# A warm-up buffer 64 bytes longer: moving two groups of tiles to another address modulo 256

## The chip, the cores and the metric

The kernel runs on one core of a Trainium2 chip. The metric is the device time of one execution in microseconds (us), lower is better. A change of less than 0.2% (1.3 us here) can hardly be told from no change.

## What is computed

A recurrent retention block feeds a SwiGLU feed-forward block. The shapes are B, H, S, D = 4, 8, 768, 64 and 3072 tokens, 512 model columns, 1536 hidden columns, all float32.

```python
for t in range(S):                      # retention, gamma by head
    state = gamma * state + k[:, :, t] (outer) v[:, :, t]
    y[:, :, t] = scale * q[:, :, t] @ state
x = y.transpose(0, 2, 1, 3).reshape(B * S, H * D)
g, val = x @ w_gate, x @ w_val
out = (g * sigmoid(g) * val) @ w_out
```

## The kernel before

**Stages.** The tokens are worked on in four segments of 768 (two halves of 384). Each segment has an attention part, an "up" part (the products with `w_gate` and `w_val`) and a "down" part (the products with `w_out`). The loops over the hidden dimension have 12 blocks `f` of 128. The first segment's up part is plain (`plain_part` L914 and `plain` L896); the three others use seven products of 128x384 for each `f` (`product`, L1062). Down is `down` (L1125): for each `f` six products, one for each token block, of 128 hidden columns by 512 output columns. While segment s is in its down stage, the attention of segment s+1 is mixed into it in twelve short blocks (`scores_of`, `mix_a`, `mix_b`, `mix_c`, all through `mm` at L766).

**Three passes to a product.** To get float32 accuracy from TensorE's float32r type, which takes one pass, operands are split by ScalarE, VectorE and GpSimd into three parts of float32r (`near_a` L967, `near_b` L970, `near_c` L973, and `far_a` to `far_c`), and each product is summed over the three parts. Those passes are the "single-pass products" of the change's title: L914, L896, L1062 and L1125. The small attention products are in float32.

**Operands and their tiles.** A pass has a stationary operand (loaded into the array, 128x128) and a moving operand (streamed past it).

| line | columns of the moving operand | moving tile | stationary tile | passes |
|---|---|---|---|---|
| L914 (`plain_part`) | 256 | `x0` | `oitem` | 144 |
| L896 (`plain`) | 384 | `x0` | `oitem` | 480 |
| L1062 (`product`) | 384 | `xa` or `xb` | `gitem`, and `oitem` for one product in seven | 1512 |
| L1125 (`down`) | 512 | `oitem` (from `w_out`) | `gitem` (the split `hT`) | 864 |

`gitem` and `oitem` come from two rings: `item` hands out the four slots g0 to g3 and the three slots o0 to o2 in turn (a `gitem` with number k lies in slot k mod 4). So in each down stage the blocks f = 2, 6 and 10 have their stationary tile in g2, and in the up stages one `gitem` in four lies there.

**Where the tiles lie.** The tiles are laid out in SBUF one after another in the order in which the program first names them, each rounded up to 32 bytes. `hT`, `x0` (its space is that of `xa`), `first` (that of `xb`), g0, g1 and g3 come first, then `loads`, `tmp`, `chunk_x`, `tab`, `local`, `last`, `states`, `warm`; o0, o1, o2 and g2 are first named later and come behind `warm`:

```python
states = consts.tile([P, 2, 2, NP, D], F32, name="states")
warm = place("warm", P + 16)
...
t = place(f"{kind}item{k}", {"g": 3 * 2 * TH, "o": 3 * DM}[kind], R12,
          tag=f"{kind}{k % slots}")
```

`warm` has 144 words (576 bytes) in each partition. It is used by the sixteen small products ahead of the work (`warm_up`, L1214). With the program's first tile at byte 16,512, the addresses modulo 256 are: `hT`, `x0`/`xa`, `first`/`xb`, g0, g1, g3: 128. o0, o1, o2 and g2 (201,536 and on): 64. All slices that the passes take start at a multiple of 512 bytes from a tile's start, so the tile's value is also the operand's.

**Order.** The order of all steps is written out by hand in `PLAN` (a list of some 2,370 names such as `3/D6.2`: segment 3, down, f = 6, token block 2); each engine works its part of that list in order. No name, wait or instruction depends on an address.

Of the kernel before, what the change touches and what calls it, by code (L numbers as in the profile page):

```python
# [17 lines left out]
P = 128  # L18
# [358 lines left out]
def tile_retnet_swiglu(  # L377
# [31 lines left out]
    def place(name, n, dtype=F32, **kw):  # L409
        return consts.tile([P, n], dtype, name=name, **kw)  # L410
# [15 lines left out]
    local = place("local", 2 * NP * HC + H + NP)  # L426
    last = place("last", 512)
    states = consts.tile([P, 2, 2, NP, D], F32, name="states")
    warm = place("warm", P + 16)

    def lay(sizes):
        at, out = 0, []
# [868 lines left out]
```

## Time and profile before

| | |
|---|---|
| time, median of 3 runs | 655.86 us (655.47 to 656.15) |
| the profiled execution | 656.0 us, of which the span from first to last instruction is 654.2 us |
| TensorE busy | 640.8 us, 98% of the span |
| granted TensorE clock, mean | 0.994 |
| VectorE, ScalarE, GpSimd busy | 490.0, 389.8, 271.4 us |

Stages on the span's clock: attention and plain up 0 to 134 us, down of segment 0 to 201, up to 291, down to 358, up to 443, down to 512, up to 599, down to the end.

In the rows below, a row of the timeline gives the start (us), the time from the first start to the last end (us), engine, line, operation, tiles, shape and count. Matmuls overlap: each record lasts from the pass's start until its results are written, so a row of n passes spans n - 1 distances between starts and one record's length.

### The profile page before, as it was taken

How to read it: one execution, taken by the hardware profiler on the slowest of the kernel's cores; microseconds unless marked ns; L12 is line 12 of the kernel's file. 1: busy time of each engine (PE TensorE's matmuls, PEld its weight loads, DVE VectorE, ACT ScalarE, POOL GpSimd, SP SyncE). 2: the span in 40 equal slices, each digit the busy share in tenths (PEclk: the TensorE clock that was granted, in tenths of full speed). 3: DMA queues.
4: the chain of work that ended last, by engine and by line, in shares of the span. 5: the costliest groups of instructions: out<-in, count | busy, mean ns of one | idle time of the engine just before them, and what ended most of it. 6: DMA issues, size and time to landing. Idle time of an engine off the chain costs nothing.

```text
span 654.2 us, 14042 instructions
## 1 busy us (share of the span) xinstructions
PE 640.8 (98%) x5576; PEld 580.7 (89%) x5576; DVE 490.0 (75%) x712; ACT 389.8 (60%) x860; POOL 271.4 (41%) x174
## 2 busy tenths in 40 slices
PE   6999999999999999999999999999999999999997
PEld 6999999977778999997778999998777999999885
DVE  4898688798898887675787868767498776778361
ACT  3688788576855555665766555555676554654211
POOL 0544356534445685730103765650103766562000
PEclk8999999999999999999999999999999999999999
DMA  9999897498867444178765640449677434304554
GB/s 325 362 350 345 320 348 275 169 370 277 272 227 277 168 145 170 33 216 258 241 232 209 205 150 15 172 151 304 189 260 251 164 142 168 115 0 162 185 201 146
DMA packets 50050, 140.13 MB, mean 214 GB/s; under 512 B 4928, under 2 KB 17472, under 8 KB 49984
## 3 DMA queue, kind: packets, MB, share of 16 engines
q1 hardware_dynamic: 49552, 138.57, 61.4%
q8 instruction: 44, 0.72, 0.4%
q10 hardware_dynamic: 432, 0.66, 0.3%
q14 instruction: 22, 0.18, 0.1%
HBM read 109.32 MB, written 29.88 MB: 213 GB/s over the span
## 4 chain that ended last, share of the span: by engine, by line
PE 87%; DVE 6%; ACT 2%; DMA 2%; issue 1%; POOL 1%; SPq 0%; ACTq 0%; DVEq 0%; POOLq 0%
PE bank L1062 40%; PE bank L1125 25%; PE bank L896 12%; PE bank L766 5%; PE bank L914 3%; ACT chunk_x L996 1%; DMA rawp<-in_w_gate_dram 1%; DVE gitem L970 1%; PE bank L721 1%; PE bank L636 1%; PE bank L692 1%; DVE oitem L983 1%; PE bank L707 1%; DVE gitem L407 1%; DVE xa L983 1%
## 5 line engine op out<-in xcount | busy, mean ns | idle before, releaser
L1125 PE MATMUL bank<-oitem,gitem 128*128 128x512 f32 x864 | 212.6, 399 | 2.8 <-DVE oitem L983 1.9
L1125 PEld LDWEIGHTS bank<-oitem,gitem 128*128 128x128 f32 x864 | 159.3, 188 | 41.8 <-DVE oitem L983 3.8
L973 POOL TENSOR_TENSOR gitem<-gitem 128x768 fp32r<-128x768 f32 x72 | 143.6, 2003 | 105.7 <-DVE gitem L970 102.9
L1062 PE MATMUL bank<-xa,gitem 128*128 128x384 f32 x864 | 162.5, 337 | 0.6 <-ACT tmp L1078 0.3
L1062 PEld LDWEIGHTS bank<-xa,gitem 128*128 128x128 f32 x864 | 150.9, 188 | 2.9 <-ACT tmp L1077 2.1
L973 POOL TENSOR_TENSOR oitem<-oitem 128x256 fp32r<-128x256 f32 (+1 forms) x60 | 66.6, 1114 | 72.8 <-DVE oitem L970 70.9
L970 DVE SCALAR_TENSOR_TENSOR gitem<-gitem,loads 128x768 fp32r<-128x768 f32 x72 | 80.8, 1139 | 14.1 <-ACT gitem L967 11.7
L967 ACT ACTIVATE gitem<-loads 128x768 fp32r<-128x768 f32 x72 | 59.3, 842 | 51.1 <-PE bank L1062 39.4
L1062 PE MATMUL bank<-xb,gitem 128*128 128x384 f32 x432 | 85.9, 336 | 0.2 <-POOL gitem L973 0.2
L896 PE MATMUL bank<-x,oitem 128*128 128x384 f32 x480 | 84.6, 337 | 0.8 <-POOL oitem L973 0.8
L896 PEld LDWEIGHTS bank<-x,oitem 128*128 128x128 f32 x480 | 82.9, 188 | 1.5 <-POOL oitem L973 1.1
L1062 PEld LDWEIGHTS bank<-xb,gitem 128*128 128x128 f32 x432 | 76.5, 188 | 1.1 <-POOL gitem L973 0.6
L970 DVE SCALAR_TENSOR_TENSOR gitem<-gitem,hT 128x768 fp32r<-128x768 f32 x48 | 49.1, 1027 | 28.1 <-ACT gitem L967 28.0
L967 ACT ACTIVATE gitem<-hT 128x768 fp32r<-128x768 f32 x48 | 39.9, 840 | 43.7 <-PE bank L1125 36.2
L996 ACT COPY chunk_x<-bank 64x128 f32<-64x128 f32 x144 | 35.4, 260 | 29.6 <-PE bank L766 20.6
L793 POOL TENSOR_TENSOR loads<-loads,tab 128x512 f32<-128x512 f32 x9 | 13.6, 1508 | 92.7 <-PE bank L766 78.5
L407 DVE SCALAR_TENSOR_TENSOR gitem<-gitem 128x768 fp32r<-128x768 f32 x48 | 46.8, 982 | 0.6
L1062 PE MATMUL bank<-xb,oitem 128*128 128x384 f32 x216 | 43.7, 338 | 0.0
L1062 PEld LDWEIGHTS bank<-xb,oitem 128*128 128x128 f32 x216 | 37.8, 188 | 0.4 <-POOL oitem L973 0.2
L970 DVE SCALAR_TENSOR_TENSOR oitem<-oitem,loads 128x256 fp32r<-128x256 f32 (+1 forms) x42 | 32.7, 783 | 3.4 <-ACT oitem L967 3.3
L979 POOL TENSOR_TENSOR oitem<-oitem 128x512 fp32r<-128x512 f32 x12 | 20.6, 1715 | 28.2 <-ACT oitem L976 20.6
L1079 DVE TENSOR_TENSOR hT<-bank,tmp 128x384 f32<-128x384 f32 x36 | 19.9, 553 | 14.7 <-PE bank L1062 14.4
(112 smaller groups left out, 787.1 us busy)
## 6 DMA issues: line engine op xcount, KB each, us to landing
loads<-wup SPq DMA_DIRECT2D x36, 896.0 KB, 4.7
oitem<-wdnt SPq DMA_DIRECT2D x36, 768.0 KB, 4.5
wdnt<-oitem SPq DMA_DIRECT2D x12, 768.0 KB, 4.6
wup<-first SPq DMA_DIRECT2D x9, 896.0 KB, 5.6
rawp<-in_w_gate_dram SPq DMA_DIRECT2D x12, 512.0 KB, 6.4
rawp<-in_w_val_dram SPq DMA_DIRECT2D x12, 512.0 KB, 5.8
rawp<-in_w_out_dram SPq DMA_DIRECT2D x12, 512.0 KB, 6.2
out_dram<-chunk_x SPq DMA_DIRECT2D x22, 256.0 KB, 2.2
```

The source lines that it names most:

```text
L407: stt(o, x, 1.0, y, op0=mul, op1=op)
L766: nc.tensor.matmul(o, a, b, start=start, stop=True, skip_group_check=True)
L896: nc.tensor.matmul(o, w[:, a, ts(b, P)], X0[:, a, i, NC - 1 - b], start=a == b == 0, stop=a == 2 and b == NC - 1, skip_group_check=True)
L914: nc.tensor.matmul(o, w[:, a, ts(b, P)], X0[:, a, :, NC - 1 - b, ts(j, P)], start=a == b == 0, stop=a == 2 and b == NC - 1, skip_group_che ...
L967: act(o[0], x, AF.Copy, scale=CUT / FAR)
L970: stt(o[1], f32(o[0]), -FAR, x, op0=mul, op1=add)
L973: op(o[2], f32(o[0]), f32(o[1]), op=add)
L979: op(o[1], f32(o[0]), x, op=sub)
L996: copy(cx[half[i], ds(2 * h, 2), c, half[z]], y.rearrange("p (b t) -> p b t", b=2))
L1062: nc.tensor.matmul(o, w[:, a, k], x[:, a, KH - 1 - k], start=start and a == k == 0, stop=a == 2 and k == KH - 1, skip_group_check=True)
L1079: lambda: copy(p5, wb), lambda: tt(h1, x, p5, op=add),
L1125: nc.tensor.matmul(banks[tok], hs[f][:, a, ds(i * TH + u * P, P)], wo[f][:, a], start=f == a == 0, stop=f == NF - 1 and a == 2, skip_group ...
```

## The change

`warm` gets 16 more words, 64 bytes, in each partition. The sixteen warm-up products and the memset that fills the buffer keep their code; the memset covers 160 words instead of 144. Everything that is laid out behind `warm` moves by 64 bytes: o0, o1, o2 and g2 go from 64 to 128 modulo 256. Nothing else changes, neither an instruction nor its order.

```diff
     states = consts.tile([P, 2, 2, NP, D], F32, name="states")
-    warm = place("warm", P + 16)
+    warm = place("warm", P + 32)
```

## The prediction, as put on record

> **What bounds the kernel now.** I read the page first, for the shares of the engines and the chain that ended last:
>
> ```profile
> span 654.2 us, 14042 instructions
> PE 640.8 (98%) x5576; PEld 580.7 (89%) x5576; DVE 490.0 (75%) x712; ACT 389.8 (60%) x860; POOL 271.4 (41%) x174
> PE 87%; DVE 6%; ACT 2%; DMA 2%; issue 1%; POOL 1%; SPq 0%; ACTq 0%; DVEq 0%; POOLq 0%
> ```
>
> TensorE (PE) is busy for 98% of the span and carries 87% of the chain. Next come the waits of PE (engine, line, what it waited for: us in total, times, longest):
>
> ```profile
> PE bank L1125 <- DVE oitem L983: 1.9, 2, 1.5
> PE bank L896 <- POOL oitem L973: 0.8, 1, 0.8
> PE bank L1062 <- ACT tmp L1078: 0.3, 1, 0.3
> ```
>
> They are small, so the time is PE's own pace: passes times the distance between the starts of two passes. The chain in order of time shows that pace over long stretches (start, us, what):
>
> ```profile
> 33.25 13.80 PE bank L914 x120
> 47.05 60.32 PE bank L896 x348
> 600.96 49.49 PE bank L1125 x213
> ```
>
> The last stage is a single run of 213 passes, 49.49 / 213 = 0.232 us each. Is that one pace, or a mixture? By the kernel's order of slots, the passes of f = 2, 6 and 10 have a moving tile (o) and a stationary tile (g2) that both lie at 64 modulo 256; in the nine other blocks the stationary tile lies at 128. In the last stage's order the 18 passes from about 625.0 us on are f = 6, and the 54 before them are other blocks. So I asked for the timeline of PE inside each:
>
> ```profile
> 612.62 12.06 PE L1125 MATMUL bank<-oitem,gitem 128*128 128x512 f32 x51
> 626.83 2.43 PE L1125 MATMUL bank<-oitem,gitem 128*128 128x512 f32 x10
> ```
>
> and for the records' lengths (minimum/median/maximum ns):
>
> ```profile
> L1125 PE MATMUL bank<-oitem,gitem x51: 393/398/398, 612.6 to 624.3; 128*128 128x512 f32 x51
> L1125 PE MATMUL bank<-oitem,gitem x10: 389/389/390, 626.8 to 628.9; 128*128 128x512 f32 x10
> ```
>
> A row of n passes spans n - 1 distances and one record. Unequal addresses: (12.06 - 0.398) / 50 = 0.2332 us. Equal addresses: (2.43 - 0.389) / 9 = 0.2268 us. Same shape, same line, same clock, nothing waiting in either: there are two paces, 6.4 ns apart, and today three quarters of the down passes (648 of 864) have the longer one. This is the observation on which the forecast rests.
>
> **The up passes (384 columns).** Here the moving tile lies at 128, g0, g1 and g3 at 128, and g2 and o at 64:
>
> ```profile
> 250.80 2.07 PE L1062 MATMUL bank<-xa,gitem 128*128 128x384 f32 x11
> 228.02 1.20 PE L1062 MATMUL bank<-xa,gitem 128*128 128x384 f32 x6
> 249.59 1.03 PE L1062 MATMUL bank<-xb,gitem 128*128 128x384 f32 x5
> 256.91 1.05 PE L1062 MATMUL bank<-xa,gitem 128*128 128x384 f32 x5
> L1062 PE MATMUL bank<-xa,gitem x864: 333/334/445, 203.6 to 598.9; 128*128 128x384 f32 x173
> ```
>
> The last row gives the record: 0.334 us. The first row is a stretch of equal addresses, (2.07 - 0.334) / 10 = 0.1736 us; the second has its stationary tile in g2, unequal, (1.20 - 0.334) / 5 = 0.1732 us. So once settled the two have one pace, and nothing is to be had from the pace itself. The third and fourth row are both five passes on equal addresses; the third comes behind another product on equal addresses, the fourth directly behind a product whose stationary tile is an `oitem` at 64. It is 0.02 us longer, and with the pass at the border itself some 0.025. A crossing from a tile at 64 to one at 128 thus costs about 25 ns, spread over four passes, after which the pace is 173 ns again. Along the order of the products there are 53 such crossings in the three up stages (17 or 18 in each). With all tiles at 128 there are none.
>
> **The change part by part.**
>
> *Down of the last segment.* All 213 passes at 0.2268: 212 x 0.2268 + 0.39 = 48.47, and a first few passes to settle, some 0.04. From 49.49 that is 1.0 us less. Behind the last pass only the last copies and stores follow, which move along.
>
> *Down of segments 1 and 2.* The same 216 passes are cut by twelve attention blocks and the borders to the up stages into some 13 runs of 16 or 17. A run must settle again after each cut. Nine passes behind a cut, first with unequal, then with equal addresses:
>
> ```profile
> 340.92 2.37 PE L1125 MATMUL bank<-oitem,gitem 128*128 128x512 f32 x9
> 302.31 2.35 PE L1125 MATMUL bank<-oitem,gitem 128*128 128x512 f32 x9
> ```
>
> Over the first nine only 0.02 us is gained, then 6.4 ns for each pass: a run of 16.6 gains 0.02 + 7.6 x 0.0064 = 0.07 us, 13 runs 0.9 us. A quarter of the passes has the good addresses already, so 0.7 us in each of the two stages, 1.4 together.
>
> *Down of segment 0.* The same sum gives 0.7. But here PE's longest wait of any stage stands (1.9 us in two times for the split of `w_out` on VectorE, the row on L1125 above; asked of 134 to 201 us alone, the view gives the same row), and VectorE is nearly full; the second row is the next down stage, for comparison (span, then busy us and count of PE, PEld, DVE, ACT, POOL):
>
> ```profile
> 134.00:201.00 67.00, 65.00 (x889) 50.06 (x888) 61.76 (x82) 46.71 (x138) 27.06 (x16) 1.00 0.84 293
> 291.00:357.90 66.90, 66.65 (x904) 53.24 (x903) 49.56 (x76) 44.08 (x130) 9.55 (x6) 1.00 0.71 239
> ```
>
> VectorE works for 61.76 of 67.00 us against 49.56 of 66.90. What PE gains ahead of such a wait is waited out again. Ends 0 and 0.7; I take 0.25, nearer to the full engine's row.
>
> *Up, three stages.* 53 x 0.025 = 1.3 us. A few crossings stand beside waits for ScalarE (0.3 us in the row on L1078), so I take 1.2; ends 0 and 1.4.
>
> *Plain up.* Stationary tiles (o) go from 64 to 128 under a moving tile at 128. For the 480 passes of 384 columns the up rows price it: 0.1736 against 0.1732, which is nothing; L896 runs at (60.32 - 0.33) / 347 = 0.1729 today. For the 144 passes of 256 columns no row has equal addresses. From the down rows it could be 6.4 ns less (144 x 0.0064 = 0.9 us gained); on the other side a crossing's 25 ns at the start of each of the twelve products would be 0.3 lost. I take 0, as the 384-column rows are the nearest in kind.
>
> *Other engines.* They write and read the moved tiles. ScalarE's first split part, into a tile at 128 (f = 5) and at 64 (f = 6):
>
> ```profile
> 609.43 0.85 ACT L967 ACTIVATE gitem<-hT 128x768 fp32r<-128x768 f32 x1 [3.34 <-PE bank L1125]
> 612.86 0.85 ACT L967 ACTIVATE gitem<-hT 128x768 fp32r<-128x768 f32 x1 [2.58 <-PE bank L1125]
> ```
>
> Equal, so 0; by the same row I take VectorE and GpSimd at 0 too. The memset of `warm` writes 160 words for 144:
>
> ```profile
> 0.84 0.18 DVE L1229 MEMSET warm<- 128x144 f32 x1 [0.84 <-PEq L1291]
> ```
>
> That is at most 0.18 x 16/144 = 0.02 us, ahead of warm-up products that run while the first loads are still on their way. No instruction is moved past another on any queue and no wait is added.
>
> *Sum.* 1.0 + 1.4 + 0.25 + 1.2 = 3.85 us. The profiled execution took 656.0 (span 654.2 and 1.8 around it), 0.14 above the median of 655.86, so the two scales agree. 656.0 - 3.85 = 652.15; I say **652.1 us**, 0.6% faster.
>
> **A rule that speaks against it.** Two paces for one shape are in the rows above, 0.2332 and 0.2268. The Trainium skill, "TensorE: Matmul & The Clock Gate", section "Step-by-step: what each phase is for", says that PE has two independent read ports into SBUF, so that loading the next stationary tile takes no bandwidth from the running pass; by that rule the relation of the two addresses could not matter and the time would stay at 656.0. The trace does not agree with the rule in its plain form. The same page's section "Back-to-back issue gap" would put a pass of 512 columns at N / 2.4 + 2.5, an estimate of 216 ns; neither measured pace is that short.
>
> **The rivals.**
>
> *No effect (656.0).* The 0.227 passes differ from the 0.233 passes in one more way: moving and stationary tile lie close together, both behind `warm` above byte 201,536, and in no other down block. If nearness, not the address modulo 256, makes them short, the change alters nothing in down, and the crossings in up (g2 and o lie far from `xa` and `xb`) stay too. For it: the rows can't separate the two. Against it: in up, tiles far apart at equal addresses run in the same settled way as anywhere, and one would expect neighbours to disturb each other rather than help. The ports rule above gives the same 656.0. Chance 0.12 for both.
>
> *Slower: the stationary tile's own address decides.* In down, the 0.227 passes also have their stationary tile at 64 and the 0.233 passes at 128. If a stationary tile at 64 is the cheap one whatever the moving tile is, the change moves every one of them to 128. Then the 216 short down passes become long, + 216 x 0.0064 = 1.4 us; the 144 passes of 256 columns, all at 64 today, may lose as much each, + 0.9; and if the 25 ns is the price of getting into work at 128 after any break, it stays, now at the breaks. 656.0 + 2.3 = 658.3. It decides at the f = 2, 6 and 10 blocks: their settled distance goes from 0.227 to 0.233. For it: the down rows fit it word for word. Against it: in up, stationary tiles at 128 and at 64 have the same settled pace. Chance 0.08.
>
> *The gain is waited out.* A faster PE reaches the other engines' results earlier. By the waits above PE idles little today, but if segment 0 gives nothing and each up stage only half, 1.0 + 1.4 + 0.6 = 3.0 remain: 653.0. This lies inside the forecast's own range.
>
> **How the numbers follow.** Chance 0.80 that the time falls by more than 0.2% (forecast and its waited-out form), 0.12 that it stays within 0.2%, 0.08 slower. The forecast's own range: all ends at their best, 1.05 + 1.4 + 0.7 + 1.4 + 0.9 = 5.45, which gives 650.5; with the first-stage, up and plain terms at their worst, 1.0 + 1.4 - 0.3 = 2.1, which gives 653.9. To leave out no more than 2 in 10, the range reaches up to the rival without effect: 650.5 to 656.0. The bound of 0.2% is about what a measurement of this kernel can tell from no change.
>
> **What would show it.** Right: in the last stage all blocks have records of 389 ns and distances of 0.227, none of 398 and 0.233; its 213 passes take 48.5 us; a product behind an `oitem` product is no longer than others; and the mean record of the whole group falls from today's 399 ns by some 6:
>
> ```profile
> L1125 PE MATMUL bank<-oitem,gitem 128*128 128x512 f32 x864 | 212.6, 399 | 2.8 <-DVE oitem L983 1.9
> ```
>
> Wrong would be: f = 0, 1, 3 still at 0.233 (no effect), f = 2, 6, 10 at 0.233 (own address), or the distances are right and PE's idle time grows by what they gained (waited out).

## The result, and the profile after

The changed kernel takes 652.64 us (median of 22 runs, 651.78 to 657.35) against 655.44 us for the kernel before (22 runs, 654.48 to 657.31). The ratio is 0.9961, with a 95% interval of 0.995 to 0.9972: 2.6 us less, between 1.8 and 3.3. The forecast was 652.1. The profiled execution took 652.16 us, with a span of 650.4; of before it was 656.0 and 654.2. The page and the waits of PE of the kernel after, in the columns known from before:

```profile
span 650.4 us, 14042 instructions
PE 636.1 (98%) x5576; PEld 579.8 (89%) x5576; DVE 490.3 (75%) x712; ACT 389.5 (60%) x860; POOL 270.9 (42%) x174
...
PE 91%; DVE 3%; DMA 2%; ACT 2%; POOL 1%; issue 1%; SPq 0%; ACTq 0%; DVEq 0%; POOLq 0%
...
L1125 PE MATMUL bank<-oitem,gitem 128*128 128x512 f32 x864 | 208.7, 395 | 3.2 <-DVE oitem L983 2.9
```

```profile
PE bank L1125 <- DVE oitem L983: 2.9, 2, 1.7
...
PE bank L766 <- DVE tmp L789: 0.6, 1, 0.6
...
PE bank L1062 <- ACT tmp L1078: 0.3, 1, 0.3
```

PE works 4.7 us less for the same 5576 instructions. The wait for the split of `w_out` (L983) has grown from 1.9 to 2.9 us, though, and a wait of 0.6 us of the small attention products (L766) for VectorE's L789 is new. The long stretches of the chain (start, us, what):

```profile
32.22 14.59 PE bank L914 x120
46.81 60.33 PE bank L896 x348
...
598.25 48.34 PE bank L1125 x213
```

The last stage, 49.49 before, is 48.34 now. Two rows of its timeline, with the records behind the first of them (minimum/median/maximum ns), stand at the places whose counterparts the prediction shows:

```profile
610.14 11.72 PE L1125 MATMUL bank<-oitem,gitem 128*128 128x512 f32 x51
623.74 2.43 PE L1125 MATMUL bank<-oitem,gitem 128*128 128x512 f32 x10
```

```profile
L1125 PE MATMUL bank<-oitem,gitem x51: 388/389/390, 610.1 to 621.5; 128*128 128x512 f32 x51
```

Both have one pace: (11.72 - 0.389) / 50 = 0.2266 us and (2.43 - 0.389) / 9 = 0.2268 us; no record of 398 ns is left among the 51. But the first row of the chain, L914, is longer than before: 14.59 us for 13.80.

The table gives the time of each stage, measured from the start of its first pass to that of the next stage's first pass (of L914 its long stretch only, between the same two passes in every kernel; of the last stage from its first pass to its last). It uses the profiled executions of both kernels and one more profiled execution of each, from the experiments below; a column gives the two.

| stage | before | after | mean change | forecast |
|---|---|---|---|---|
| plain up, 256 columns (L914) | 13.49, 14.01 | 14.28, 14.28 | +0.53 | 0 |
| plain up, 384 columns (L896) | 87.34, 87.34 | 87.36, 87.35 | 0.0 | 0 |
| down of segment 0 | 67.30, 67.71 | 67.97, 67.99 | **+0.48** | -0.25 |
| up, segment 1 | 90.14, 89.77 | 89.66, 89.66 | -0.30 | -0.4 |
| down of segment 1 | 66.46, 66.60 | 65.70, 65.84 | -0.76 | -0.7 |
| up, segment 2 | 84.99, 85.00 | 84.58, 84.58 | -0.41 | -0.4 |
| down of segment 2 | 68.30, 68.62 | 66.95, 68.06 | -0.96 | -0.7 |
| up, segment 3 | 89.36, 89.36 | 89.22, 89.18 | -0.16 | -0.4 |
| down of segment 3 | 49.24, 49.24 | 48.09, 48.09 | -1.15 | -1.0 |
| sum | | | -2.7 | -3.85 |

The sum of -2.7 agrees with the -2.6 to -2.8 of the medians. The two executions of before differ by 0.37 us in the up stage of segment 1; they part between 214 and 219 us, where the first waits 0.2 us for GpSimd (L973) and the second does not. What comes ahead of these stages is left out: it varied between 31.6 and 33.5 us from execution to execution.

### The profile page after: what moved, and what is told of

The parts are those of the page before. It is cut to its first block, busy times and chain, and to the rows that moved or that the text cites. A ratio compares the mean times of both kernels' runs of the same rounds, so it can differ in the third digit from the quotient of the medians.

```text
span 650.4 us, 14042 instructions
## 1 busy us (share of the span) xinstructions
PE 636.1 (98%) x5576; PEld 579.8 (89%) x5576; DVE 490.3 (75%) x712; ACT 389.5 (60%) x860; POOL 270.9 (42%) x174
## 4 chain that ended last, share of the span: by engine, by line
PE 91%; DVE 3%; DMA 2%; ACT 2%; POOL 1%; issue 1%; SPq 0%; ACTq 0%; DVEq 0%; POOLq 0%
PE bank L1062 40%; PE bank L1125 29%; PE bank L896 12%; PE bank L766 5%; PE bank L914 3%; DMA rawp<-in_w_gate_dram 1%; PE bank L636 1%; PE bank L707 1%; ACT chunk_x L996 1%; PE bank L721 1%; POOL oitem L973 1%; PE bank L692 1%; DMA loads<-in_k_n_dram 0%; POOL gitem L973 0%; DMA oitem<-wdn 0%
## 5 line engine op out<-in xcount | busy, mean ns | idle before, releaser
L1125 PE MATMUL bank<-oitem,gitem 128*128 128x512 f32 x864 | 208.7, 395 | 3.2 <-DVE oitem L983 2.9
L973 POOL TENSOR_TENSOR gitem<-gitem 128x768 fp32r<-128x768 f32 x72 | 143.4, 2001 | 105.2 <-DVE gitem L970 102.5
L973 POOL TENSOR_TENSOR oitem<-oitem 128x256 fp32r<-128x256 f32 (+1 forms) x60 | 66.6, 1114 | 72.3 <-DVE oitem L970 63.7
L970 DVE SCALAR_TENSOR_TENSOR gitem<-gitem,loads 128x768 fp32r<-128x768 f32 x72 | 80.8, 1138 | 13.9 <-ACT gitem L967 10.0
L896 PE MATMUL bank<-x,oitem 128*128 128x384 f32 x480 | 84.6, 336 | 0.8 <-POOL oitem L973 0.8
L896 PEld LDWEIGHTS bank<-x,oitem 128*128 128x128 f32 x480 | 83.0, 188 | 1.5 <-POOL oitem L973 1.1
L970 DVE SCALAR_TENSOR_TENSOR gitem<-gitem,hT 128x768 fp32r<-128x768 f32 x48 | 48.3, 1012 | 26.7 <-ACT gitem L967 26.6
L793 POOL TENSOR_TENSOR loads<-loads,tab 128x512 f32<-128x512 f32 x9 | 13.7, 1522 | 90.9 <-PE bank L766 90.9
L970 DVE SCALAR_TENSOR_TENSOR oitem<-oitem,loads 128x256 fp32r<-128x256 f32 (+1 forms) x42 | 32.8, 786 | 3.7 <-ACT oitem L967 3.6
```

Of the source, the lines that this page charges most:

```text
L896: nc.tensor.matmul(o, w[:, a, ts(b, P)], X0[:, a, i, NC - 1 - b], start=a == b == 0, stop=a == 2 and b == NC - 1, skip_group_check=True)
L970: stt(o[1], f32(o[0]), -FAR, x, op0=mul, op1=add)
L973: op(o[2], f32(o[0]), f32(o[1]), op=add)
L1125: nc.tensor.matmul(banks[tok], hs[f][:, a, ds(i * TH + u * P, P)], wo[f][:, a], start=f == a == 0, stop=f == NF - 1 and a == 2, skip_group ...
```

## Experiments

Two questions stood open. Is it the relation of the two addresses that sets the pace, or a tile's own address, or the nearness of the tiles? And why does the down stage of segment 0 lose time although its passes have become shorter? In what follows, "distance" is the moving address minus the stationary one, modulo 256.

**The change once more (after2).** The kernel after, for a second trace and more runs.

> The changed kernel once more, with a second profile. Theory (equal addresses modulo 256 shorten the down passes, remove the crossings in up, and lengthen the 256-column passes): the same distances as in the first profile, 0.2268 us on L1125, 0.120 us on L914; a ratio to the kernel before of about 0.996. What the first profile gained before the first L914 pass (1.1 us) and lost in the down stage of segment 0 (0.7 us): if they belong to the change they come again, that is 17.7 us up to the first L914 pass and 68.0 us for that down stage; if they are chance, the values scatter around those of before, 18.8 and 67.3 us.

It took 653.41 us (6 runs) where the kernel before took 655.97 (11 runs, shared by the first four experiments): ratio 0.9962, 0.9948 to 0.9976. All stages agree with the first trace but one: down of segment 2 took 68.06 for 66.95. The difference is a single pass near 459 us, to which a later paragraph comes back.

**The tiles behind `warm` left at 64, the others brought there (apart).** Here g0, g1 and g3 move to 64, and o and g2 are at 64 as they were before the change. Moving and stationary tiles of down are equal again, but at 64, and `x0`, `xa`, `xb` stay at 128.

```diff
     first = place("first", XB, tag="xb")
+    tab = place("tab", NTAB)
+    local = place("local", 2 * NP * HC + H + NP)
+    warm = place("warm", P + 16)
     rawp = {i: place(f"rawp{i}", 3 * 2 * TH, tag=f"g{i}") for i in (0, 1, 3)}
...
-    tab = place("tab", NTAB)
-    local = place("local", 2 * NP * HC + H + NP)
...
-    warm = place("warm", P + 32)
```

> No longer warm-up buffer; instead tab, local and warm are laid out ahead of the g tiles, so that all g and o tiles lie at 64 modulo 256 while hT, xa, xb and x0 stay at 128. Down passes then have equal addresses in all blocks, plain and up passes unequal ones. Theory (the relation of the two operands counts): L1125 at 0.2268 us in all blocks as in the changed kernel; up at 0.1733 us without crossings, since all stationary tiles lie at 64; L914 back at 0.1133 us, 0.9 us less than in the changed kernel. Time 651.7, ratio to before 0.9945. Rival (stationary tile at 128 is what counts): L1125 all at one of the two paces for another reason, up as before; rival (only the place behind the small tiles counts, tiles close together): L1125 as before at 0.2332 in f other than 2, 6, 10, time 655.

It took 652.55 us (7 runs), ratio 0.9946 (0.9931 to 0.996). L914 did not go back to 0.113 us, as was expected; more on that with before2. Blocks f = 6 and f = 7 of its last stage, 16 passes each, with stationary tiles in g2 and g3:

```profile
626.19 3.79 PE L1125 MATMUL bank<-oitem,gitem 128*128 128x512 f32 x16
...
630.27 3.79 PE L1125 MATMUL bank<-oitem,gitem 128*128 128x512 f32 x16
```

(3.79 - 0.389) / 15 = 0.2267 us in both: the short pace at 64 as at 128. With the trace of after, where stationary tiles at 128 run at 0.2266, this refutes the rival of the own address. Nearness falls too: in after the short pace holds for g0, g1 and g3, which lie far from the o tiles.

**Other distances (off128, off192, off96).** In off128 `warm` is as before and `local` is laid out ahead of the g tiles, so g0, g1 and g3 lie at 192, o and g2 at 64: distance 128. In off192 the o tiles and g2 lie at 192, the other g tiles at 128: distance +64. In off96 the former lie at 96: distance -32. The edits of off192 and off96 are shown against the kernel after.

```diff
# off128 (against the kernel before)
     first = place("first", XB, tag="xb")
+    local = place("local", 2 * NP * HC + H + NP)
     rawp = {i: place(f"rawp{i}", 3 * 2 * TH, tag=f"g{i}") for i in (0, 1, 3)}
...
-    local = place("local", 2 * NP * HC + H + NP)
# off192
-    warm = place("warm", P + 32)
+    warm = place("warm", P + 48)
# off96
-    warm = place("warm", P + 32)
+    warm = place("warm", P + 24)
```

> Kernel before with only local moved ahead of the g tiles: g0, g1, g3 lie at 192 modulo 256, o and g2 at 64, xa, xb, x0 at 128. Down passes have operands 128 apart in nine blocks and equal ones in f = 2, 6, 10. Theory (equality modulo 256): 0.2332 us on L1125 in the nine blocks, 0.2268 in f = 2, 6, 10; no pair in up is equal, so no crossing, 1.3 us less there; time about 654. Rival (equality modulo 128 is enough): 0.2268 us in all blocks, time about 651.5.

> Kernel before with warm 128 bytes longer: o and g2 at 192 modulo 256, so the distance of moving and stationary tile has the other sign: +64 in down where before had -64, and -64 in up and plain where before had +64. Theory (equality modulo 256): L1125 at 0.2332 us in f other than 2, 6, 10; L1062 with crossings, 53 x 25 ns; L914 at 0.1133 us; time as before, 655.4. Rival (the sign counts: the moving tile behind the stationary one is the free case): L1125 at 0.2268 us in all blocks and a slower L914, time about 652.

> Kernel before with warm 32 bytes longer: o and g2 at 96 modulo 256, so down has a distance of -32, up and plain of +32 where before had -64 and +64. Theory as an all-or-nothing equality: L1125 at 0.2332 us in f other than 2, 6, 10, as at -64. Theory as a graded distance: between 0.2268 and 0.2332. Time 654 to 655.5.

One run of each: 656.92, 655.82 and 657.81 us. Beside off96 a single run of the kernel before took 659.17, and before2, the same kernel, took 655.72, so single times decide nothing here; the paces do. Block f = 5 of the last stage in off128, off192 and off96, in this order:

```profile
622.22 3.88 PE L1125 MATMUL bank<-oitem,gitem 128*128 128x512 f32 x16
```

```profile
621.54 3.83 PE L1125 MATMUL bank<-oitem,gitem 128*128 128x512 f32 x16
```

```profile
623.03 3.89 PE L1125 MATMUL bank<-oitem,gitem 128*128 128x512 f32 x16
```

With a record of 0.389 to 0.398 us at the end that is 0.232 us, 0.229 us and 0.233 us. The blocks f = 2, 6, 10, equal in all three kernels, stay at 0.227. So neither "the same address modulo 128" nor "any distance but 64" will do: equality modulo 256 gives the shortest pace, +64 costs 2 ns and -64 (the kernel before) 6 ns. The expectation of 0.233 for off192 was wrong here: the sign counts. But +64 has a second pace. Blocks f = 0 and 1 of the same stage of off192 run at (6.22 - 0.39) / 25 = 0.233 us, and 0.229 sets in only from f = 2 on:

```profile
602.22 6.22 PE L1125 MATMUL bank<-oitem,gitem 128*128 128x512 f32 x26
```

In off192 the 384-column passes of L896 show a further price, which the prediction's rows could not show. First off192, then after:

```profile
49.70 30.55 PE L896 MATMUL bank<-x,oitem 128*128 128x384 f32 x172
```

```profile
49.77 30.49 PE L896 MATMUL bank<-x,oitem 128*128 128x384 f32 x175
```

(30.55 - 0.336) / 171 = 0.1767 us with distance -64, (30.49 - 0.336) / 174 = 0.1733 us with distance 0, and 0.173 with +64 in the kernel before. Its whole stage grows from 87.36 to 88.58 us. off96 (distance +32 there) has 88.55. In off128 the 1.3 us expected from up did not come: its three up stages take 89.82, 84.96 and 89.38 us, as in the kernel before. A product behind an `oitem` takes 1.048 us there (median) for 1.062 in before, but those on g0, g1 and g3 among themselves take 1.047 for 1.040.

**The kernel before once more, and o alone (before2, only_o).** before2 is the kernel before. In only_o the o tiles lie at 128 as after the change, but g2 stays at 64, so that three quarters of the down passes become equal and f = 2, 6, 10 get distance +64. Against the kernel after:

```diff
-    warm = place("warm", P + 32)
+    warm = place("warm", P + 16)
+    place("ahead", 3 * 2 * TH, tag="g2")
+    place("pad", 16)
```

> The kernel before once more, for a second profile. In its first profile L914 ran at 0.1133 us in its long stretch and at 0.1177 in two short ones, and in two other kernels with unequal addresses (off128, off192) it runs at 0.1177 throughout. If 0.1133 belongs to this layout, it comes again and the change costs 0.8 us there; if it is one of two paces that the stretch falls into by chance, 0.1177 may come, and the change costs 0.3 us there. The down stage of segment 0: 67.3 us again. The stop of PE near 459 us: any value from 0.6 to 2.8 us beside the pass, as it varies in the five other profiles.

> Half of the change: o0, o1, o2 moved to 128 modulo 256, g2 left at 64 (g2 is laid out first behind warm, then 64 bytes of padding, then the o tiles). Theory (the distance of the two operands modulo 256 sets the pace): the nine blocks other than f = 2, 6, 10 at 0.2268 us settled, f = 2, 6, 10 now with a distance of +64, as in off192, mean 0.230 us. In up only products behind g2 have a crossing left, a third of the 53. Last stage 48.1 + 54 x 0.003 = 48.3 us. Rival (the tile's own place): f = 2, 6, 10 stay at 0.2268.

One run of each: 655.72 and 652.49 us. Blocks f = 6 (now unequal) and f = 7 (now equal) of only_o; the lines of its file are shifted by two:

```profile
622.42 3.83 PE L1127 MATMUL bank<-oitem,gitem 128*128 128x512 f32 x16
626.54 3.79 PE L1127 MATMUL bank<-oitem,gitem 128*128 128x512 f32 x16
```

The pattern of the kernel before is turned round: f = 6 at 0.229, f = 7 at 0.227. The last stage, in the table's measure, took 48.21 us for 48.09 of after. The pace follows the pair of tiles, not the block.

before2 also answers for L914. Part of its long stretch in the kernel before, in before2, after and apart:

```profile
34.77 10.48 PE L914 MATMUL bank<-x,oitem 128*128 128x256 f32 x91
```

```profile
34.81 10.41 PE L914 MATMUL bank<-x,oitem 128*128 128x256 f32 x87
```

```profile
34.77 10.48 PE L914 MATMUL bank<-x,oitem 128*128 128x256 f32 x86
```

```profile
34.76 10.41 PE L914 MATMUL bank<-x,oitem 128*128 128x256 f32 x87
```

With a record of 0.28 us they run at (10.48 - 0.28) / 90 = 0.113, 0.118, 0.120 and 0.118 us. The first, second and fourth have the same addresses (distance +64), so that distance has two paces, 0.113 or 0.118, which one execution or another of the same kernel showed; of the five executions with these addresses (off128 and apart_both too) only the first of before ran this stretch at 0.113. Equal addresses gave 0.120 in both traces of after. only_o has both distances in one execution: one of the four `oitem`s of L914 lies in g2 (+64), the three others at 128 (equal). The first row below has equal addresses, the second has those in g2:

```profile
34.72 3.04 PE L916 MATMUL bank<-x,oitem 128*128 128x256 f32 x24
38.07 2.66 PE L916 MATMUL bank<-x,oitem 128*128 128x256 f32 x22
```

(3.04 - 0.28) / 23 = 0.120 us and (2.66 - 0.28) / 21 = 0.113 us. In L914 equality is thus the longest pace, not the shortest. These passes differ from those of down in more than their 256 columns, though: their moving operand is two runs of 128 columns (`X0[:, a, :, NC - 1 - b, ts(j, P)]`). Which of the two turns the order round no run shows.

**Segment 0: GpSimd's scaling taken off VectorE's back (relieve).** PE waits there for VectorE, so its order was followed through the stage. At one place the two kernels part: from the start of the first to that of the last of thirteen operations of VectorE that follow one another are 8.54 us in both traces of before, and in off128, off192, off96 and only_o, but 9.14 us in after, after2 and apart. Behind that place PE waits the new 0.6 us for L789, which of these nine traces only the last three show. First the kernel before at that place, then after:

```profile
175.52 0.41 DVE L407 SCALAR_TENSOR_TENSOR tmp<-tmp,chunk_x 128x256 f32<-128x256 f32 x1
175.57 1.51 POOL L793 TENSOR_TENSOR loads<-loads,tab 128x512 f32<-128x512 f32 x1 [3.94 <-PE bank L766]
175.85 2.06 DVE L970 SCALAR_TENSOR_TENSOR gitem<-gitem,hT 128x768 fp32r<-128x768 f32 x1
```

```profile
175.11 1.30 POOL L793 TENSOR_TENSOR loads<-loads,tab 128x512 f32<-128x512 f32 x1 [3.83 <-PE bank L766]
175.17 1.52 DVE L407 SCALAR_TENSOR_TENSOR tmp<-tmp,chunk_x 128x256 f32<-128x256 f32 x1
176.61 1.79 DVE L970 SCALAR_TENSOR_TENSOR gitem<-gitem,hT 128x768 fp32r<-128x768 f32 x1
```

GpSimd's scaling of q (L793) is released by PE. Before, it started just behind VectorE's short operation, which took 0.41 us. After, the sooner PE lets it start 0.06 us ahead of that operation, which then takes 1.52 us. In only_o and off192 GpSimd's record starts first too, but by 0.02 us, and VectorE's operation keeps its 0.42 us. The theory is that GpSimd's operation holds VectorE's up, and that this, not the addresses, makes the stage longer. The experiment does this one scaling with the helper that puts it on VectorE, on top of the change:

```diff
-    def scale_q2(p, i):
+    def scale_q2(p, i, here=pool):
...
-        (pool if i else both)(t, t, qdec, op=mul)
+        (here if i else both)(t, t, qdec, op=mul)
...
-    at(d + 0.2 + 0.1 * i, f"{nxt}/q{p}.{i}", scale_q2, p, i)
+    at(d + 0.2 + 0.1 * i, f"{nxt}/q{p}.{i}", scale_q2, p, i, both if nxt == 1 and p == 2 else pool)
```

> The changed kernel with one step moved from GpSimd to VectorE in the down stage of segment 0: the scaling of q of the third pair (1/q2.1, L793). Theory (the 0.6 to 0.7 us that the stage loses come from a GpSimd instruction that starts 0.1 us earlier relative to VectorE and holds up one more VectorE instruction): no VectorE instruction of 256 columns at 175 us is stretched from 0.42 to 1.52; VectorE has 0.68 us more work and two stretches of 1.1 us less; the stage takes 67.2 to 67.5 us against 68.0 of the changed kernel. Rival (the stage is longer for another reason, say DMA): it stays at 68.0 or gets longer by the added 0.68.

One run, 651.33 us. The same two operations of VectorE, and GpSimd's next step:

```profile
174.85 0.42 DVE L407 SCALAR_TENSOR_TENSOR tmp<-tmp,chunk_x 128x256 f32<-128x256 f32 x1
175.19 0.95 DVE L970 SCALAR_TENSOR_TENSOR gitem<-gitem,hT 128x768 fp32r<-128x768 f32 x1
...
170.92 1.05 POOL L798 TENSOR_TENSOR tmp<-tmp,local 128x512 f32<-128x512 f32 x1
```

And the whole stage (span, busy us and count of PE, PEld, DVE, ACT, POOL), after and relieve:

```profile
134.01:201.98 67.97, 64.51 (x889) 50.49 (x889) 62.84 (x83) 46.48 (x135) 26.48 (x16) 1.00 0.82 289
```

```profile
133.72:199.93 66.21, 64.22 (x889) 50.28 (x889) 61.25 (x84) 46.81 (x137) 24.43 (x15) 1.00 0.84 293
```

VectorE does one operation more (84 for 83) and is busy for 1.6 us less; the stage falls from 67.97 to 66.21 us, 1.3 us below the mean of before. It brought more than the 0.6 us lost at this place and more than was expected (67.2 to 67.5): GpSimd's next operation (L798) no longer stands behind the scaling, and L970, which took 2.06 and 1.79 us in the rows above, now takes 0.95. The kernel before with the same edit was not run, so how much of the 1.8 us it would gain as well is open.

**The pass near 459 us (late).** In every trace one pass of the down stage of segment 2, near 459 us, always the same one, stops in mid-product for nothing that the profile shows: from its start to the next pass's it takes from 0.65 to 2.79 us over all the traces of this study. It was longest in the profiled execution of apart, whose PE timeline is shown with the transfer of instructions that ran then:

```profile
458.54 0.73 PE L1125 MATMUL bank<-oitem,gitem 128*128 128x512 f32 x2
461.67 3.40 PE L1125 MATMUL bank<-oitem,gitem 128*128 128x512 f32 x10 [2.40 <-issue]
```

```profile
q8 instruction: 2, 0.03, 2.2%
```

In every trace a packet of this queue (16,384 bytes) ends 1.2 to 1.7 us before PE goes on, however long the stop is. Is it held up by the load `3/l11`, which the order places there? In late that load comes some 40 steps later in the order written out by hand:

```diff
-    ... 2/D4.4 3/l11 2/D4.3 ...
+    ... 2/D4.4 2/D4.3 ...
...
-    ... 2/W7 3/x0.0.0 ...
+    ... 2/W7 3/l11 3/x0.0.0 ...
```

> The changed kernel with one load of the last segment's attention (3/l11, three transfers, 0.5 MB) issued some 17 us later, behind 2/W7. It tests where the run-to-run scatter of the down stage of segment 2 comes from (66.95 to 70.55 us in ten profiles, with one stop of PE near 459 us of 0.6 to 2.8 us for which no semaphore is shown). Theory: PE waits there for its next instructions, whose transfer (queue q8, a packet within the microsecond before the stop's end) stands behind the loads issued from 450 to 455 us. With 0.5 MB less ahead of it the stop is 0.5 us or less and the stage takes 66.0 to 66.7 us. Rival: the stop has nothing to do with the loads; it stays within 0.6 to 2.8.

One run, 653.67 us. The spot in late:

```profile
459.18 0.73 PE L1125 MATMUL bank<-oitem,gitem 128*128 128x512 f32 x2
460.40 2.43 PE L1125 MATMUL bank<-oitem,gitem 128*128 128x512 f32 x10 [0.49 <-issue]
```

The pass lasted 0.89 us, where 0.5 or less was expected, well within the scatter of the others. The load is not shown to be the cause, and the cause stays open; the steady time from the transfer of instructions to the end of the stop points at it, but no run changed it. The stop is in before as in after (1.21 and 1.05 us in the two traces of before, 0.65 and 1.75 in those of after), so it makes scatter and not the difference.

**The best version (both, apart_both).** The change with the edits of relieve and late, and apart with the same two.

> The changed kernel with both: q of the third pair on VectorE in the first down stage (relieve) and the later load (late). Sum of the parts against the changed kernel: 1.8 us (relieve's 66.2 against 68.0 in that stage) and some 1.0 us (the stop near 459). Time some 650.5 beside a kernel before of 655.9, ratio 0.992. Rival: relieve's gain was a chance of its one profile; then ratio 0.9945.

> The layout of apart (g and o at 64, xa, xb, x0 at 128) with the same two edits. apart had 0.3 us less than the changed kernel in L914 and 0.3 us less in the three up stages: time some 649.9, ratio 0.991. Rival: the layouts are equal in time within the interval.

They took 651.53 us (5 runs, 651.12 to 652.99; ratio 0.9941, 0.9928 to 0.9953) and 651.34 us (5 runs, 651.16 to 652.7; ratio 0.994, 0.9927 to 0.9954) against 655.89 (9 runs). In both the down stage of segment 0 is short again, 66.40 and 66.43 us, which confirms relieve's stage twice. The times are 4.4 and 4.5 us below the kernel before. The ratios of 0.992 and 0.991 that were expected did not come: the stop near 459 us lasted 0.93 and 1.47 us, so late brought nothing. By the ratios, both is about 1.3 us below the change alone (0.9941 against 0.9961), but the two intervals overlap a little. both and apart_both can't be told apart.

## Why the prediction was right, step by step

*Two paces, set by the pair of addresses: right.* Once settled, all blocks run at 0.227, and only_o, apart and the three other distances show that the pair decides. What lay behind was wider than the step said: the paces are graded (0.227, 0.229, 0.232, 0.233), and -64 was among the worst. Of the signs named, the mean record of all down passes fell by 4 ns (399 to 395) and not by some 6.

*Down of the last segment: right.* 48.34 us on the chain, 48.47 forecast.

*Down of segments 1 and 2: right in kind, a little low.* -0.76 and -0.96 for -0.7 each; the two traces of after differ by 1.1 us in segment 2 through the pass near 459 us, so the second figure says little.

*Down of segment 0: wrong in sign.* The step took the gain as waited out at worst, with ends of 0 and 0.7 gained. The stage got 0.48 us longer. The passes did give what the sum said: PE is busy there for 65.30 and 65.01 us in the two traces of before, and for 64.51 and 64.49 in those of after. Its waits took more than that back. The one on L983 is 2.9 us in both traces of after, but before it was 1.9 or 2.7:

```profile
PE bank L1125 <- DVE oitem L983: 2.7, 2, 1.5
```

This row is from before2, so the growth of 1.0 us seen in the first pair of traces is in part the scatter of before. The 0.6 us on L789 comes from the collision: a PE that is ahead also releases GpSimd sooner, and that operation ran into VectorE, on which PE then waits. only_o, without the collision, has no such wait and a stage of 67.39 us. The lower end should have reached below nothing: an engine that is full can lose through others' earlier starts.

*Up: right in kind, too high.* 53 crossings at 0.025 should have given 1.3 us, of which the step took 1.2; it was 0.30 + 0.41 + 0.16 = 0.87. The spot from which the price was read, in after:

```profile
256.02 1.20 PE L1062 MATMUL bank<-xb,oitem 128*128 128x384 f32 x6
257.06 1.03 PE L1062 MATMUL bank<-xa,gitem 128*128 128x384 f32 x5
```

The five passes behind an `oitem` product take 1.03 us for 1.05, as forecast. Over all products behind a crossing the median fell from 1.063 to 1.040 us, some 22 ns each, but the mean from 1.068 only to 1.050: some crossings gave nothing (one product took 1.148 us in all four traces). In segment 3 six products even got 13 to 25 ns longer, for a reason that stays open. Two stops for ScalarE there (0.31 and 0.26 us idle) are the same in before, after and apart, so they don't explain it.

*Plain up: the mis-sized term.* The step took 0 with ends of -0.9 and +0.3 for the 256-column passes, by the 384-column rows. It was +0.53 on average: the pace went from 0.113 or 0.118 to 0.120 us over some 120 passes. Against the first trace of before the loss is 0.79 us, far beyond the upper end; against before2, whose pace is the usual one, it is 0.27, inside the range. The missing row mattered: these passes go the other way than those of 512 columns.

*Other engines and the memset: 0, as said* (VectorE, ScalarE and GpSimd are busy for 490.3, 389.5 and 270.9 us, before 490.0, 389.8 and 271.4), but for the collision above, which comes from the moment of a start and not from an address: apart, with other addresses, has it too.

*The sum.* 3.85 forecast, 2.7 by the stages. The 1.1 between is made of segment 0 (0.73), plain up (0.53) and up (0.33 less than forecast), with the other down stages giving 0.47 more. That the forecast of 652.1 lies only 0.5 from the measured 652.64 is in part luck: it starts from the one profiled execution of 656.0, while the median of before is 655.44. The gain of 3.85 itself lies outside the measured 1.8 to 3.3.

*The ports rule.* The Trainium skill, "TensorE: Matmul & The Clock Gate", "Step-by-step: what each phase is for", gives loads of the stationary operand a read port of their own. These runs do not agree with the conclusion that the prediction drew from it, that the relation of the two addresses could not matter: with the same instructions the pace depends on the pair by up to 6.6 ns of 227. Whether it is the load that slows the running pass they do not show.

## What to carry to other kernels

For a PE-bound stream of single-pass float32r products, look at the moving and the stationary tile's address modulo 256: padding one small tile was worth 6 ns a pass at 512 columns here, but measure each form of pass, since the passes of 256 columns (two runs of 128) lost time by equality. When an engine on the critical path gets ahead, ask what it releases on the others and whose operation that will meet; 0.6 us of the waits in segment 0 came from there, and moving one operation to another engine brought back 1.8 us where the collision had cost 0.6. Price a term on the form of pass it runs on, or leave its range wide. And take two traces of the kernel before: its own stages differed by up to 0.5 us.

## What was not expected of the hardware

The settled distance between passes, by the distance of addresses (ns; a dash was not measured):

| moving minus stationary, modulo 256 | 512 columns | 384 columns | 256 columns |
|---|---|---|---|
| 0 | 227 | 173 | 120 |
| +64 | 229, or 233 at first | 173 | 113 or 118 |
| -64 | 233 | 177 | 118 |
| 128 | 232 | - | - |
| +32 | - | 177 | - |
| -32 | 233 | - | - |

No run explains the order of these rows. The 256 columns are two runs of 128. A VectorE operation of 0.41 us became one of 1.52 us when an operation of GpSimd had started 0.06 us ahead of it. And in the profiled execution of apart, after PE had stood for 2.4 us near 459 us, its granted clock fell. The windows from there on (span, busy us and count of five engines, granted clock):

```profile
458.80:461.60 2.80, 0.47 (x2) 0.22 (x2) 0.00 (x0) 2.71 (x11) 0.00 (x0) 1.00 0.23 52
461.60:463.00 1.40, 1.33 (x6) 1.06 (x6) 0.00 (x0) 0.43 (x2) 0.00 (x0) 0.97 0.06 13
463.00:465.00 2.00, 2.00 (x5) 1.05 (x4) 0.00 (x0) 0.00 (x0) 0.00 (x0) 0.50 0.00 0
465.00:467.00 2.00, 2.00 (x51) 1.86 (x51) 0.00 (x0) 0.00 (x0) 0.00 (x0) 0.67 0.00 0
```

The clock was 0.97 in the first 1.4 us of work, then 0.50 for 2 us and 0.67 in the next 2, and four passes followed one another 0.427 us apart, not 0.227. From the pass that ends the stop to the 62nd matmul behind it apart took 5.81 us and after2 4.28, so the stop of 2.8 us cost about another 1.5 us. After the stops of 1.75 us in after2 and 2.26 us in off128 the clock stayed at 1.00.
